# Attention queries loaded without their zeros, and the first weights' clamp on GpSimd

## The chip, the cores and the metric

The kernel runs on one core of a Trainium2 chip. The metric is the device time of one execution in microseconds. The kernel before takes 577.83 us (median of three runs, 577.48 to 578.81).

## The reference

Eight batches go through an attention with a local mask and then through a layer that mixes tokens and channels.

```python
B, H, S, D = 8, 8, 576, 64
scores = q @ k.T / sqrt(D)          # per batch and head
mask: heads 0-3: 0 <= i - j < 32;  heads 4-7: 0 <= i - j < 128 and (i - j) % 4 == 0
attn = softmax(where(mask, scores, -1e9));  o = attn @ v
x = o.transpose(0, 2, 1, 3).reshape(B, S, 512)
theta = x @ w_theta                 # 512 x 512
zr, zi = x * cos(theta), x * sin(theta)
u = x + (w_tok_r @ zr + w_tok_i @ zi)   # over the 576 tokens
out = u + max(u @ w_ch, 0)
```

The mixing weights come as 64-bit numbers and are turned into float32 on the chip.

## The kernel before, in words

**Tiling.** The eight heads of a batch are handled as four pairs. The heads with the dilated mask have their tokens reordered on the host, so that every head sees a window of 32 tokens. A pair's 576 queries are 18 blocks of 32; a block of queries meets the 64 keys of its own block and the one before. One score matmul does a block for both heads of the pair: the keys of the two heads lie on partitions 0 to 63 and 64 to 127, 64 columns of them stream, and the stationary operand is a tile of 128 partitions by 64 columns that holds head 0's 32 queries in its upper left quarter, head 1's in its lower right quarter, and zeros elsewhere. The result has the queries of the two heads on 64 partitions, and even and odd blocks use the two halves of the array's columns. In float32 each matmul becomes two instructions of TensorE, and each of them a weight load (PEld) and a stream (PE), so a pair has 36 of each.

**The zeros.** The host writes the zeros into the array qT (1001 to 1010), and every load of a pair's queries brings them along: 128 partitions by 1152 numbers, 576 KB, of which half are zeros. The queries of batch 0 go into four tiles that are later used for something else (278, 282); those of the other batches into a pool of two buffers (218, 221), 28 loads of them.

**Weights.** `unpack` (311 to 345) makes float32 of a 64-bit weight tile, whose 32-bit halves lie interleaved, so that each operation steps 8 bytes: a clamp of the upper half on VectorE (332), a scaling on ScalarE (334), a shift or scaling of the lower half (337 or 340), and a merge on VectorE (342). `split` (347) then makes a high part on ScalarE and a low part on GpSimd (352). The weights that are unpacked with `early` set are the four tiles of w_theta (st_wth) and the five of the first half of the token weights (st_wtk, g = 0). The second token half and w_ch come later, with `early` false.

**The stages.** Batch 0's attention comes first, then theta (667), the cosines and sines, and the token and channel units (850, 882). From batch 1 on, a batch's token and channel matmuls run beside the next batch's scores (468), probabilities (504 to 510), transposes (525), products with v (617) and theta (685). The low parts `zl` of the rotated tokens (646) are made on GpSimd.

**Order.** The work of batch 0 and the beginning of batch 1 is put in order by a small planner (`Order`, 62 to 125): each step names an engine and a cost in ns, and steps of a lower rank go first. The engines run what it emits in that order, each in its own queue. So a cost or an engine that a step names also moves the steps around it. From batch 1's units on, the order is written out by hand (`phase`, 889) and doesn't depend on costs. All loads and stores are issued by SyncE (SP), one after the other.

Of the kernel before, what the change touches and what calls it, by code (L numbers as in the profile page):

```python
# [8 lines left out]
F32 = mybir.dt.float32  # L9
# [5 lines left out]
ALU = mybir.AluOpType  # L15
PSUM = bass.MemoryType.PSUM

B, H, S, D = 8, 8, 576, 64
DM = H * D
NP = H // 2  # L20
QB = 32
BW = 2 * QB
NJ = S // (2 * QB)
# [35 lines left out]
W_MAX = 2.0 ** 16 * (2.0 - 2.0 ** -3)  # L59


class Order:
# [13 lines left out]
    def pin(self, ins):  # L76
        if self.live:
            self.tc.keep_in_program_order(ins)

    def signal(self, event):  # L80
        self.events[event] = self.now
# [53 lines left out]
def dve2(n):  # L135
    return 67 + 0.52 * n


def act(n):
    return 95 + 0.83 * n  # L140
# [6 lines left out]
def dma(n):  # L147
    return 128 * 4 * n / 360.0
# [3 lines left out]
def build(ctx, tc, qT, kT, vw, wth, wtk, wch, maskb, ident, identb, outT):  # L152
    nc = tc.nc
    cp = ctx.enter_context(tc.tile_pool(name="const", bufs=1))
    ap = ctx.enter_context(tc.tile_pool(name="attn", bufs=2))
# [12 lines left out]
    pin, go, signal = od.pin, od.go, od.signal  # L168

    def pe(ins):  # L170
        tc.keep_in_program_order(ins)
# [17 lines left out]
    def take(tag, bufs, n=None):  # L189
        n = reserve(tag) if n is None else n  # L190
        if od.live:
            if n >= bufs:
                yield None, ("free", tag, n - bufs)
            if n:
                yield None, ("got", tag, n - 1)
            signal(("got", tag, n))
        return n
# [15 lines left out]
    def load_qk(n):  # L213
        if n >= B * NP:
            return
        b, pr = divmod(n, NP)
        r = yield from take("qk", 2)
        q = ap.tile([128, 2 * NJ, 2 * QB], F32, tag="q", name=f"q{b}_{pr}")
        k = ap.tile([128, S + 32], F32, tag="k", name=f"k{b}_{pr}")
        yield "DMA", dma(2 * S)  # L220
        pin(nc.sync.dma_start(q, qT[b, pr]))
        yield "DMA", dma(S + 32)
        pin(nc.sync.dma_start(k, kT[b, pr]))
        qks[b, pr] = (q, k, r)
        signal(("qk", b, pr))

    def load_va(n):
        if n >= B * NP:
            return
        b, pr = divmod(n, NP)  # L230
        r = yield from take("va", 2)
        va = ap.tile([128, VA, 128], F32, tag="va", name=f"va{b}_{pr}")
        yield "DMA", dma(VA * 128)
        pin(nc.sync.dma_start(va, vw[b, pr, :, :VA]))
        vs["a", b, pr] = (va, r)
        signal(("va", b, pr))

    def load_vb(n):
# [12 lines left out]
        vs["b", b, pr] = (vb, r)  # L251
        signal(("vb", b, pr))

    KE = S + 32
    first_k = hp.tile([128, 10 * HS], F32R, tag="wt_b", name="first_k").bitcast(F32)
    first_v = hp.tile([128, 8 * HS], F32R, tag="wt_a", name="first_v").bitcast(F32)
# [13 lines left out]
    def first_loads():  # L270
        yield "DMA", dma(3 * BW + 64)
        pin(nc.sync.dma_start(mskb, maskb.bitcast(BF16)))
        pin(nc.sync.dma_start(idb, identb.bitcast(BF16)))
        for pr in range(NP):
            yield from take(f"xh{pr}", 1, 0)
            yield from take(f"u{pr}", 1, 0)
            pqs.append(hp.tile([128, 2, S], F32R, tag=f"xh{pr}", name=f"P0_{pr}").bitcast(F32)[:, 0])
            q = hp.tile([128, 2, S], F32R, tag=f"u{pr}", name=f"q0_{pr}").bitcast(F32)
            q = q.rearrange("p a b -> p (a b)").rearrange("p (a b) -> p a b", b=2 * QB)
            k = first_k[:, KE * pr:KE * pr + KE]  # L280
            yield "DMA", dma(2 * S)
            pin(nc.sync.dma_start(q, qT[0, pr]))
            yield "DMA", dma(KE)
            pin(nc.sync.dma_start(k, kT[0, pr]))
            qks[0, pr] = (q, k, None)
            if pr == 0:
                yield "DMA", dma(128)
                pin(nc.sync.dma_start(idt, ident))
            signal(("qk", 0, pr))
        for pr in range(NP // 2):  # L290
            v = first_v[:, NJ * 128 * pr:NJ * 128 * pr + NJ * 128].rearrange("p (a b) -> p a b", b=128)
            yield "DMA", dma(NJ * 128)
            pin(nc.sync.dma_start(v, vw[0, pr]))
            for h, t in (("a", v[:, :VA]), ("b", v[:, VA:])):
                vs[h, 0, pr] = (t, None)
                signal(("v" + h, 0, pr))
        for pr in range(NP // 2, NP):
            yield from load_va(pr)
            yield from load_vb(pr)

    def consts():
        yield "DVE", 60
        pin(nc.vector.memset(halfpi, math.pi / 2))
        for n in range(2):
            t = cp.tile([128, NJ, 2, 2 * QB], F32, name=f"pt{n}")
            yield "POOL", 1040
            pin(nc.gpsimd.memset(t, 0.0))
            pts.append(t)
        signal("pts")

    def unpack(src, sz, name, stage, early, n, key):

        tag = None
        if stage is None:
            st = hp.tile([128, 2 * DM], F32R, tag=f"wc{n}", name=f"st_{name}{n}")
        else:
            tag = stage
            yield from take(tag[0], 1, tag[1])
            st = hp.tile([128, 2, S], F32R, tag=tag[0], name=f"st_{name}{n}").rearrange("p a b -> p (a b)")
        raw = st[:, :2 * sz].bitcast(U32)  # L320
        yield "DMA", dma(2 * sz)
        if len(src.shape) == 3:
            pin(nc.sync.dma_start(raw.rearrange("p (c b) -> p c b", c=src.shape[1]), src.bitcast(U32)))
        else:
            pin(nc.sync.dma_start(raw, src.bitcast(U32)))
        signal(("raw", name, n))
        yield None, ("raw", name, n)
        pair = raw.rearrange("p (a b) -> p a b", b=2)
        Ci, Ti = pair[:, :, 1], pair[:, :, 0]
        C, T = Ci.bitcast(F32), Ti.bitcast(F32)  # L330
        yield "DVE", dve2(sz)
        pin(nc.vector.tensor_scalar(C, C, W_MAX, -W_MAX, op0=ALU.min, op1=ALU.max))
        yield "ACT", act(sz)
        pin(nc.scalar.activation(C, C, AF.Prelu, scale=2.0 ** -112, alpha=-2.0 ** 32))
        if early and n % 2 == 0:
            yield "DVE", dve2(sz)
            pin(nc.vector.tensor_scalar(Ti, Ti, 29, None, op0=ALU.logical_shift_right))
        else:
            yield "ACT", act(sz)
            pin(nc.scalar.activation(Ti, Ti, AF.Copy, scale=2.0 ** -29, bias=-0.5))  # L340
        yield "DVE", dve(sz)
        pin(nc.vector.scalar_tensor_tensor(out=Ti, in0=Ci, scalar=3, in1=Ti,
                                           op0=ALU.logical_shift_left, op1=ALU.bitwise_or))
        signal(key)
        return T, tag
# [95 lines left out]
    def scores(b, pr):  # L441
# [3 lines left out]
        if pr >= 1:  # L445
            yield None, ("sc", b, pr - 1)
        q, k, rqk = qks[b, pr]
        if b == 0:
            P, rp = pqs[pr].rearrange("p (a b) -> p a b", b=BW), None
        else:  # L450
            rp = yield from take("P", 2)
            P = sp.tile([128, NJ, BW], F32, tag="P", name=f"P{b}_{pr}")
# [3 lines left out]
        for g0, g1 in ((0, 5), (5, NJ)):  # L456
            ps, rel = yield from bank("s", f"s{b}_{pr}_{g0}")
            ps = ps[:, :(g1 - g0) * BW].rearrange("p (a b) -> p a b", b=BW)
            held[g0] = ps, rel
            masked = on_pe(b, pr)  # L460
            if masked:
                yield "PE", 150
                mask_on_pe(ps, pr, g0, g1)
            yield "PE", 162 * (g1 - g0)
            for n in range(g0, g1):
                for e in range(2):
                    qb = 2 * n + e
                    pe(nc.tensor.matmul(ps[64 * e:64 * e + 64, n - g0], q[:, qb],
                                        k[:, QB * qb:QB * qb + BW], start=not masked, stop=not masked or n == g1 - 1))
            if masked:  # L470
                go(row_max(b, ps, rel, P, mx, g0, g1, ("mask", b, pr, g0)))
            else:
                go(mask_scores(ps, rel, P, mx, pr, g0, g1, ("mask", b, pr, g0)))
# [521 lines left out]
def _arrays(inp):  # L995
    import numpy as np
    q, k, v = inp["q"], inp["k"], inp["v"]
# [5 lines left out]
        return a  # L1003

    q, k, v = perm(q), perm(k), perm(v)
    qT = np.zeros((B, NP, 2, D, 2 * NJ, 2, QB), q.dtype)
    qh = q.reshape(B, NP, 2, 2 * NJ, QB, D).transpose(0, 1, 2, 5, 3, 4)
    for hh in range(2):
        qT[:, :, hh, :, :, hh] = qh[:, :, hh]
    qT = qT.reshape(B, NP, 128, 2 * NJ, 2 * QB)  # L1010
    kT = np.zeros((B, NP, 128, S + 32), k.dtype)
    kT[..., 32:] = k.transpose(0, 1, 3, 2).reshape(B, NP, 128, S)
    vp = np.zeros((B, H, S + 32, D), v.dtype)
# [11 lines left out]
    for n, (j, bound) in enumerate(((1, 0), (0, 0), (2, 144), (4, 288), (6, 432), (7, 432))):  # L1025
        for quad in range(4):
            qb = 2 * j + quad // 2
            p = QB * qb + np.arange(QB)[:, None]
# [30 lines left out]
```

## Time and profile before

The profiled execution took 577.82 us, of which the span of its trace is 576.0 us; the 1.82 us around it is start and end.

| | |
|---|---|
| median of the runs | 577.83 us |
| profiled execution | 577.82 us, span 576.0 us, granted TensorE clock 0.988 |
| TensorE | streams 550.5 us (96%), weight loads 501.6 us (87%) |
| VectorE, ScalarE, GpSimd | 378.0, 345.2, 222.2 us |
| DMA | 81.91 MB in 45586 packets, 142 GB/s over the span |

In the rows of the profile, PE is TensorE's stream and PEld its weight load, which overlap; DVE is VectorE, ACT ScalarE, POOL GpSimd, SPq the issue of a DMA by SyncE. A group's row gives line, engine, operation, output<-inputs, shapes and count, then the busy time in us and the mean of one in ns, then the idle time ahead of it and what ended that. A row of the timeline begins with its start and length in us.

### The profile page before, as it was taken

How to read it: one execution, taken by the hardware profiler on the slowest of the kernel's cores; microseconds unless marked ns; L12 is line 12 of the kernel's file. 1: busy time of each engine (PE TensorE's matmuls, PEld its weight loads, DVE VectorE, ACT ScalarE, POOL GpSimd, SP SyncE). 2: the span in 40 equal slices, each digit the busy share in tenths (PEclk: the TensorE clock that was granted, in tenths of full speed). 3: DMA queues.
4: the chain of work that ended last, by engine and by line, in shares of the span. 5: the costliest groups of instructions: out<-in, count | busy, mean ns of one | idle time of the engine just before them, and what ended most of it. 6: DMA issues, size and time to landing. Idle time of an engine off the chain costs nothing.

```text
span 576.0 us, 13996 instructions
## 1 busy us (share of the span) xinstructions
PE 550.5 (96%) x5464; PEld 501.6 (87%) x5464; DVE 378.0 (66%) x1156; ACT 345.2 (60%) x939; POOL 222.2 (39%) x206
## 2 busy tenths in 40 slices
PE   5997799999999999999999999999999999999997
PEld 4744688879999899988999899988999899989997
DVE  3879798865666668756776768756775767445112
ACT  1498967768555784369555785359556695266110
POOL 2228855525224352226324253226323353325220
PEclk9999699899999999999999999999999999999999
DMA  8991437601747046540746146550747123321002
GB/s 303 400 368 28 165 105 245 216 0 63 231 150 193 32 162 210 169 127 20 268 143 172 64 148 202 181 136 11 252 146 190 69 83 102 77 89 65 18 1 83
DMA packets 45586, 81.91 MB, mean 142 GB/s; under 512 B 3920, under 2 KB 19024, under 8 KB 45520
## 3 DMA queue, kind: packets, MB, share of 16 engines
q1 hardware_dynamic: 45520, 81.02, 43.7%
q8 instruction: 43, 0.70, 0.5%
q14 instruction: 23, 0.19, 0.1%
HBM read 64.49 MB, written 16.52 MB: 141 GB/s over the span
## 4 chain that ended last, share of the span: by engine, by line
DVE 34%; ACT 30%; PE 25%; issue 5%; POOL 2%; DMA 2%; SPq 0%; ACTq 0%; POOLq 0%; DVEq 0%
DVE pt L525 16%; PE y L850 11%; ACT P L504 11%; PE c L882 6%; PE th L685 3%; DVE P L409 3%; ACT K L698 3%; ACT K L787 3%; DVE xh L599 3%; ACT th L796 2%; ACT zh L644 2%; DVE xq L729 2%; DVE K L789 2%; ACT cos L705 2%; ACT x L581 2%
## 5 line engine op out<-in xcount | busy, mean ns | idle before, releaser
L830 POOL TENSOR_TENSOR u<-x,u 128x288 fp32r<-128x288 f32 x64 | 54.7, 858 | 184.6 <-ACT u L828 184.6
L525 DVE STREAM_TRANSPOSE pt<-P 32x288 f32<-32x288 f32 x224 | 105.1, 469 | 12.0 <-POOL P L510 8.9
L882 PE MATMUL c<-u,late_wc 128*128 128x288 f32 x768 | 110.2, 296 | 2.8 <-DVE x L859 2.8
L882 PEld LDWEIGHTS c<-u,late_wc 128*128 128x128 f32 x768 | 106.0, 188 | 6.8 <-DVE x L859 4.0
L850 PE MATMUL y<-wtkh,zh 128*128 128x288 f32 x288 | 90.3, 314 | 1.1 <-ACT zh L644 1.1
L850 PE MATMUL y<-wtkh,zl 128*128 128x288 f32 x288 | 86.2, 299 | 4.0 <-POOL zl L646 4.0
L646 POOL TENSOR_TENSOR zl<-g,zh 128x512 fp32r<-128x512 f32 x40 | 52.3, 1316 | 97.5 <-ACT zh L644 84.5
L504 ACT ACTIVATE P<-P,mx 128x64 f32<-128x64 f32 x216 | 72.0, 335 | 25.8 <-DVE mx L498 25.8
L850 PE MATMUL y<-wtkl,zh 128*128 128x288 f32 x288 | 85.9, 298 | 0.0
L828 ACT CAST u<-x 128x288 fp32r<-128x288 f32 x64 | 26.9, 429 | 86.2 <-DVE x L825 85.5
L685 PE MATMUL th<-wthh,xh 128*128 128x512 f32 x224 | 74.8, 395 | 0.3 <-DVE g L784 0.3
L850 PE MATMUL y<-late_wt_b,zh 128*128 128x288 f32 x320 | 68.1, 297 | 0.0
L825 DVE TENSOR_TENSOR x<-y,x 128x288 f32<-128x288 f32 x64 | 28.1, 448 | 53.6 <-PE y L850 53.5
L850 PEld LDWEIGHTS y<-wtkh,zl 128*128 128x128 f32 x288 | 55.1, 191 | 4.7 <-POOL zl L646 4.7
L850 PEld LDWEIGHTS y<-wtkh,zh 128*128 128x128 f32 x288 | 54.9, 191 | 4.7 <-ACT zh L644 2.3
L850 PE MATMUL y<-late_wt_a,zh 128*128 128x288 f32 x256 | 56.3, 301 | 0.0
L850 PEld LDWEIGHTS y<-wtkl,zh 128*128 128x128 f32 x288 | 55.1, 191 | 0.3 <-issue 0.3
L510 POOL TENSOR_TENSOR P<-P,sm 128x576 f32<-128x576 f32 x32 | 37.5, 1172 | 41.1 <-DVE sm L508 18.1
L850 PEld LDWEIGHTS y<-late_wt_b,zh 128*128 128x128 f32 x320 | 51.4, 189 | 0.3
L685 PEld LDWEIGHTS th<-wthh,xh 128*128 128x128 f32 x224 | 42.0, 188 | 9.2 <-DVE g L784 0.6
L850 PE MATMUL y<-late_wt_b,zl 128*128 128x288 f32 x160 | 47.4, 296 | 0.0
L581 ACT COPY x<-o 128x576 f32<-128x576 f32 x32 | 29.4, 919 | 28.4 <-PE o L617 19.1
(108 smaller groups left out, 1106.3 us busy)
## 6 DMA issues: line engine op xcount, KB each, us to landing
q<-in_qT_dram SPq DMA_DIRECT2D x32, 576.0 KB, 5.2
va<-in_vw_dram SPq DMA_DIRECT2D x30, 320.0 KB, 3.2
k<-in_kT_dram SPq DMA_DIRECT2D x28, 304.0 KB, 5.5
out_dram<-x SPq DMA_DIRECT2D x28, 288.0 KB, 2.4
vb<-in_vw_dram SPq DMA_DIRECT2D x29, 256.0 KB, 3.8
xd<-xq SPq DMA_DIRECT2D x24, 288.0 KB, 5.1
xn<-xd SPq DMA_DIRECT2D x24, 256.0 KB, 3.4
st_wtk<-in_wtk_dram SPq DMA_DIRECT2D x8, 576.0 KB, 8.8
```

Source lines behind the costliest of these rows:

```text
L409: pin(nc.vector.tensor_tensor_reduce(out=P[:, n], in0=ps[:, n - g0], in1=mskb[:, mask_of(pr, n)], op0=ALU.add, op1=ALU.max, scale=1.0, sca ...
L504: table(nc.scalar.activation(P[:, n], P[:, n], AF.Exp, bias=mx[:, n:n + 1], scale=SCALE, accum_out=sm[:, n:n + 1]))
L510: pin(nc.gpsimd.tensor_tensor(P, P, sm.unsqueeze(2).to_broadcast([128, NJ, BW]), op=ALU.mult))
L525: pin(nc.vector.transpose(pmats[b, pr][k0:k0 + QB, :, hh, QB * e:QB * e + QB], P[p0:p0 + QB, :, QB * o:QB * o + QB]))
L581: pin(nc.scalar.copy(dst, src))
L646: pin(nc.gpsimd.tensor_tensor(lo, z, hi.bitcast(F32), op=ALU.subtract))
L685: pe(nc.tensor.matmul(pt, l, r, start=(n == 0), stop=(n == 3 * NC - 1)))
L825: pin(nc.vector.tensor_tensor(x[:, ts], ps, x[:, ts], op=ALU.add))
L828: pin(nc.scalar.copy(uh[b, d][:, ts], x[:, ts]))
L830: pin(nc.gpsimd.tensor_tensor(ul[b, d][:, ts], x[:, ts], uh[b, d][:, ts].bitcast(F32), op=ALU.subtract))
L850: pe(nc.tensor.matmul(ps, l[:, cs], r, start=(n == 0), stop=(n == 3 * NK - 1)))
L882: pe(nc.tensor.matmul(ps, l[:, cs], r[:, ts], start=(n == 0), stop=(n == 3 * NC - 1)))
```

## The change

It has two parts.

**Queries.** The host writes qT without zeros. A head's row holds for each of its 64 dimensions the 576 queries in the order "place in the block, then block". A pair's load is now two DMAs of 64 partitions by 576 numbers, one for each head, and each goes to its own half of a tile of 128 by 2 by 576. The other half of either partition range is set to zero by a memset: for batch 0's four tiles by VectorE just ahead of the loads, for two tiles that are now kept for all other batches by GpSimd, once. The score matmul's stationary operand is column `qb` of every group of 18: 64 columns that lie 72 bytes apart, where they were next to each other before.

**Clamp.** In `unpack`, the clamp of the nine early tiles is done by GpSimd with the planner's cost 1.2 ns an element, and no longer by VectorE.

```diff
 def load_qk(n):
-        q = ap.tile([128, 2 * NJ, 2 * QB], F32, tag="q", name=f"q{b}_{pr}")
+        q = qbufs[r % 2]
         k = ap.tile([128, S + 32], F32, tag="k", name=f"k{b}_{pr}")
-        yield "DMA", dma(2 * S)
-        pin(nc.sync.dma_start(q, qT[b, pr]))
+        yield "DMA", dma(S)
+        for hh in range(2):
+            rs = slice(64 * hh, 64 * hh + 64)
+            pin(nc.sync.dma_start(q[rs, hh], qT[b, pr, rs]))
...
+    qbufs = [cp.tile([128, 2, S], F32, name=f"q{n}") for n in range(2)]
...
 def first_loads():
-            q = q.rearrange("p a b -> p (a b)").rearrange("p (a b) -> p a b", b=2 * QB)
+            for hh in range(2):
+                pin(nc.vector.memset(q[64 * hh:64 * hh + 64, 1 - hh], 0.0))
-            yield "DMA", dma(2 * S)
-            pin(nc.sync.dma_start(q, qT[0, pr]))
+            yield "DMA", dma(S)
+            for hh in range(2):
+                rs = slice(64 * hh, 64 * hh + 64)
+                pin(nc.sync.dma_start(q[rs, hh], qT[0, pr, rs]))
...
 def consts():
         signal("pts")
+        for q in qbufs:
+            for hh in range(2):
+                yield "POOL", 580
+                pin(nc.gpsimd.memset(q[64 * hh:64 * hh + 64, 1 - hh], 0.0))
...
 def unpack(src, sz, name, stage, early, n, key):
-        yield "DVE", dve2(sz)
-        pin(nc.vector.tensor_scalar(C, C, W_MAX, -W_MAX, op0=ALU.min, op1=ALU.max))
+        if early:
+            yield "POOL", 1.2 * sz
+            pin(nc.gpsimd.tensor_scalar(C, C, W_MAX, -W_MAX, op0=ALU.min, op1=ALU.max))
+        else:
+            yield "DVE", dve2(sz)
+            pin(nc.vector.tensor_scalar(C, C, W_MAX, -W_MAX, op0=ALU.min, op1=ALU.max))
...
 def scores(b, pr):
         q, k, rqk = qks[b, pr]
+        q = q.rearrange("p h (r n) -> p (h r) n", n=2 * NJ)
...
-                    pe(nc.tensor.matmul(ps[64 * e:64 * e + 64, n - g0], q[:, qb],
+                    pe(nc.tensor.matmul(ps[64 * e:64 * e + 64, n - g0], q[:, :, qb],
...
 def _arrays(inp):
+    qT = q.reshape(B, H, 2 * NJ, QB, D).transpose(0, 1, 4, 3, 2).reshape(B, NP, 128, S)
```

How the rows move is seen at three places. The first is GpSimd's queue from its first multiplications of probabilities on (P; the number after the name is the pair, the last one only a serial number). Before:

```order
L307 MEMSET pt_109 128x1152
L510 ISA
L510 TENSOR_TENSOR P_0_104<-P_0_104,sm_0_117 128x576
L510 TENSOR_TENSOR P_1_114<-P_1_114,sm_1_148 128x576
L510 TENSOR_TENSOR P_2_121<-P_2_121,sm_2_183 128x576
L510 TENSOR_TENSOR P_3_154<-P_3_154,sm_3_227 128x576
L352 TENSOR_TENSOR wtkl_516<-st_wtk_0_149,wtkh_515 128x576
```

Now, with the change's own line numbers (323 is the memset of the kept query tiles, 347 the clamp, 529 the multiplication, 370 the low part):

```order
L317 MEMSET pt_112 128x1152
L323 MEMSET q_90 64x576 x2
L323 MEMSET q_91 64x576 x2
L529 TENSOR_TENSOR P_1_118<-P_1_118,sm_1_167 128x576
L347 TENSOR_SCALAR st_wth_98<-st_wth_98 128x512
L529 TENSOR_TENSOR P_2_129<-P_2_129,sm_2_202 128x576
L347 TENSOR_SCALAR st_wth_99<-st_wth_99 128x512
L529 TENSOR_TENSOR P_3_152<-P_3_152,sm_3_246 128x576
L347 TENSOR_SCALAR st_wth_100<-st_wth_100 128x512
L347 TENSOR_SCALAR st_wth_101<-st_wth_101 128x512
L347 TENSOR_SCALAR st_wtk_0_168<-st_wtk_0_168 128x576
```

Clamps now stand between the multiplications of the pairs, and each waits in this queue for its tile's DMA.

The second place is VectorE's queue behind the last pair's scores of batch 0, before:

```order
L332 TENSOR_SCALAR st_wth_96<-st_wth_96 128x512
L495 TENSOR_REDUCE sm_3_227<-P_3_154 128x9
L536 COPY pt_107<-pT_2_0_355 64x10x32
L536 COPY pt_107<-pT_2_5_389 64x8x32
L337 TENSOR_SCALAR st_wth_96<-st_wth_96 128x512
L507 TENSOR_SCALAR sm_3_227<-sm_3_227 128x9
L508 RECIPROCAL sm_3_227<-sm_3_227 128x9
L342 SCALAR_TENSOR_TENSOR st_wth_96<-st_wth_96 128x512
L332 TENSOR_SCALAR st_wth_97<-st_wth_97 128x512
L332 TENSOR_SCALAR st_wth_98<-st_wth_98 128x512
```

And now (355 is the shift, 360 the merge, 514 the sum of a row):

```order
L355 TENSOR_SCALAR st_wth_98<-st_wth_98 128x512
L360 SCALAR_TENSOR_TENSOR st_wth_98<-st_wth_98 128x512
L514 TENSOR_REDUCE sm_3_246<-P_3_152 128x9
L555 COPY pt_110<-pT_2_0_375 64x10x32
L526 TENSOR_SCALAR sm_3_246<-sm_3_246 128x9
L527 RECIPROCAL sm_3_246<-sm_3_246 128x9
L555 COPY pt_110<-pT_2_5_413 64x8x32
L360 SCALAR_TENSOR_TENSOR st_wth_99<-st_wth_99 128x512
```

The clamps are gone, and the first weight tile's merge stands ahead of the last pair's sum.

The third place is the head of SyncE's queue. Before:

```order
L282 DMA q_0_105<-in_qT_dram 128x1152
L284 DMA first_k<-in_kT_dram 128x608
L288 DMA idt<-in_ident_dram 128x128
L282 DMA q_1_115<-in_qT_dram 128x1152
L284 DMA first_k<-in_kT_dram 128x608
```

Now:

```order
L292 DMA q_0_106<-in_qT_dram 64x576 x2
L294 DMA first_k<-in_kT_dram 128x608
L298 DMA idt<-in_ident_dram 128x128
L292 DMA q_1_119<-in_qT_dram 64x576 x2
L294 DMA first_k<-in_kT_dram 128x608
```

The order of the tiles stays, and two smaller DMAs stand for each load of queries.

More of the change, by code (lines that the diff above doesn't have):

```diff
@@ L1005, in _arrays @@
     q, k, v = perm(q), perm(k), perm(v)
[L1006 to L1010, printed above, removed]
+    qT = q.reshape(B, H, 2 * NJ, QB, D).transpose(0, 1, 4, 3, 2).reshape(B, NP, 128, S)
     kT = np.zeros((B, NP, 128, S + 32), k.dtype)
```

## The prediction

> **What bounds the kernel now.** The page's first part and its row of DMA come first, then the busy time by stretches (length, then PE, PEld, DVE, ACT, POOL, with the granted clock, the share of DMA and GB/s at the end).
>
> ```profile
> PE 550.5 (96%) x5464; PEld 501.6 (87%) x5464; DVE 378.0 (66%) x1156; ACT 345.2 (60%) x939; POOL 222.2 (39%) x206
> DMA  8991437601747046540746146550747123321002
> ```
>
> ```profile
> 0.00:20.00 20.00, 12.88 (x220) 10.58 (x220) 8.40 (x23) 3.52 (x6) 4.38 (x8) 1.00 0.89 330
> 20.00:40.00 20.00, 18.14 (x259) 10.71 (x260) 16.04 (x34) 15.29 (x26) 4.72 (x5) 1.00 1.04 398
> 40.00:60.00 20.00, 16.09 (x86) 8.62 (x84) 18.83 (x43) 17.83 (x32) 14.79 (x11) 0.94 0.29 96
> ...
> 62.00:143.00 81.00, 74.44 (x694) 66.73 (x692) 63.44 (x145) 61.49 (x183) 44.22 (x38) 0.94 0.36 121
> 143.00:508.40 365.40, 362.62 (x3729) 341.07 (x3729) 248.23 (x868) 223.06 (x655) 134.11 (x129) 1.00 0.47 142
> ```
>
> Two kernels lie behind one average. From 143 us on TensorE is busy 362.6 of 365.4 us, and the others have a third free: only what TensorE itself does counts there. Before that it waits. DMA is full for 40 us, VectorE is busy 18.83 of 20 us from 40 to 60, ScalarE 17.83. The chain that ended last, in its first part, names the steps.
>
> ```profile
> 3.53 6.60 DMA first_k<-in_kT_dram
> ...
> 23.41 0.82 DVE st_wth L332
> ...
> 26.94 1.30 DVE st_wth L332
> ...
> 32.59 0.41 DVE st_wth L332
> ```
>
> A load of keys holds the start up to 10.13 us, and three pieces of the clamp (line 332) lie on the chain, 0.82 + 1.30 + 0.41 = 2.53 us. So the change touches both regimes: loads and clamps in the start, and the stationary operand of the scores where TensorE is the bound. The sums are made against the profiled execution, 577.82 us (span 576.0, 1.82 around it); the median of the runs, 577.83, is the same.
>
> **Term 1, the first loads.** The DMA view (KB each, then us to landing) and the timeline:
>
> ```profile
> q<-in_qT_dram SPq DMA_DIRECT2D x32, 576.0 KB, 5.2
> first_k<-in_kT_dram SPq DMA_DIRECT2D x4, 304.0 KB, 7.3
> idt<-in_ident_dram SPq DMA_DIRECT2D x1, 64.0 KB, 4.5
> ```
>
> ```profile
> 7.03 1.34 PE L468 MATMUL s<-first_k,q 128*64 128x64 f32 x20 [3.62 <-DMA first_k<-in_kT_dram]
> 8.62 1.12 PE L468 MATMUL s<-first_k,q 128*64 128x64 f32 x16
> 10.27 1.34 PE L468 MATMUL s<-first_k,q 128*64 128x64 f32 x20
> ```
>
> From the first pair's keys (scores start at 7.03) to the second's (landed at 10.13) came idt, q and k, 64 + 576 + 304 = 944 KB in 3.1 us, 305 KB a us. Half of a q is 288 KB, 0.94 us. The first scores gain at most that, the second pair's keys twice that, 1.9 us; but TensorE is at the first pair until 9.74, so a second 0.94 can't all be used. Nothing shown moves 64 partitions of q, so the lower end is 0. I take 0.9, the first pair's share, with 0 and 1.9 as ends. SyncE issues one more DMA a pair, some 0.4 us each in the start, beside transfers that are longer.
>
> **Term 2, the clamps.** VectorE loses nine operations:
>
> ```profile
> L332 DVE TENSOR_SCALAR st_wth<-st_wth 128x512 f32<-128x512 f32 x4 | 3.1, 793 | 0.0
> L332 DVE TENSOR_SCALAR st_wtk<-st_wtk 128x576 f32<-128x576 f32 x8 | 5.2, 654 | 0.0
> L332 DVE TENSOR_SCALAR st_wtk<-st_wtk 128x288 f32<-128x288 f32 x2 | 2.9, 1456 | 0.0
> ```
>
> Four of 793 ns, four of 654 and one of at most 1456 are 7.2 us, the upper end of the gain. On the chain they were 2.53 us. What is late next is ScalarE, which follows the clamp with line 334 and has only 20 - 17.83 = 2.17 us free from 40 to 60. So I take 2.0; the lower end is 0, if ScalarE's other work simply fills the place. I assume that what is gained by 60 us is carried to 143 us, since the steps between are the same and hang on one another, and from there to the end, since TensorE then only starts its full stretch earlier.
>
> **What hides at no cost.** The memsets have no row of their own size, so these bound them:
>
> ```profile
> 8.40 0.49 DVE L430 TENSOR_REDUCE mx<-s 128x5 f32<-128x320 f32 x1 [7.54 <-PE s L468]
> 13.67 1.15 POOL L510 TENSOR_TENSOR P<-P,sm 128x576 f32<-128x576 f32 x1 [10.89 <-DVE sm L508]
> L307 POOL MEMSET pt<- 128x1152 f32 x2 | 2.1, 1058 | 0.3 <-POOLq L1045 0.3
> L495 DVE TENSOR_REDUCE sm<-P 128x9 f32<-128x576 f32 x4 | 3.0, 748 | 0.4 <-ACT P L493 0.4
> ```
>
> GpSimd writes zeros at 1058 / 1152 = 0.92 ns a column, 0.53 us for 576. VectorE's eight take 4.2 us by that and 6.0 us at the 748 ns of a whole reduction; VectorE is idle from 0.86 to 8.40, and the first scores need only the first two. GpSimd's four (2.1 us) lie in 10.89 us of idle time. Both cost 0; without that cover, 4 us and 2 us.
>
> GpSimd's nine clamps lie between a memset's rate, 0.47 us for 512, and a two-input operation of the same size:
>
> ```profile
> L646 POOL TENSOR_TENSOR zl<-g,zh 128x512 fp32r<-128x512 f32 x40 | 52.3, 1316 | 97.5 <-ACT zh L644 84.5 <-issue 7.4 <-DVE zh L641 5.6
> L352 POOL TENSOR_TENSOR wtkl<-st_wtk,wtkh 128x576 fp32r<-128x576 f32 x4 | 6.0, 1512 | 10.1 <-ACT wtkh L350 10.1
> ```
>
> They are 4 to 12 us in all. I take 0.7 us each, 6.3 us, nearer the memset, as one operand is read. They come while GpSimd waits, 10.1 us in one piece ahead of line 352, so they cost nothing while the data are there in time; the case where they aren't is a rival.
>
> **Term 3, the stationary operand.** Each of the 28 pairs of batches 1 to 7 has 36 loads, whose columns will lie 72 bytes apart.
>
> ```profile
> L882 PEld LDWEIGHTS c<-u,late_wc 128*128 128x128 f32 x768 | 106.0, 188 | 6.8 <-DVE x L859 4.0
> L617 PEld LDWEIGHTS o<-pt,va 128*64 128x64 f32 x600 | 20.2, 137 | 5.8 <-issue 5.1 <-ACT pt L539 0.8
> L882 PE MATMUL c<-u,late_wc 128*128 128x288 f32 x768 | 110.2, 296 | 2.8 <-DVE x L859 2.8
> L685 PE MATMUL th<-wthh,xh 128*128 128x512 f32 x224 | 74.8, 395 | 0.3 <-DVE g L784 0.3
> ```
>
> ```profile
> 469.01 1.13 PEld L468 LDWEIGHTS s<-k,q 128*64 128x64 f32 x36 [0.16 <-ACT cos L705]
> 155.33 0.64 ACT L581 COPY x<-o 128x576 f32<-128x576 f32 x1 [4.68 <-PE o L617]
> 173.56 1.19 ACT L581 COPY x<-o 128x576 f32<-128x576 f32 x1
> ```
>
> A load of 64 columns less is 188 - 137 = 51 ns shorter, 0.80 ns a column. A stream takes (395 - 296) / (512 - 288) = 0.44 ns a column. The 36 loads start within 1.13 - 0.14 = 0.99 us, every 28.4 ns (the last one's 0.14 taken off), so about two of 51 ns run at a time, and the streams set the pace. No row has columns apart in a stationary operand. TensorE is seen to fetch a number of 4 bytes in 0.44 ns, and a load asks for one in 0.80: a fetch at half the rate would still keep up. On ScalarE the same 576 numbers take 0.64 us when written side by side (pairs 0 and 1) and 1.19 us when written 16 bytes apart (pairs 2 and 3), so something in the memory does cost 1.9 times. The ends are thus 0 and a doubled load; I take 0, since TensorE's own rows are nearer than another engine's write, and keep the other end as the first rival.
>
> The sum: 577.82 - 0.9 - 2.0 + 0 = **574.9 us**. Its own range, with half of term 2's upper end, is 571 to 577.
>
> **Rivals.**
>
> 1. **The loads of apart columns are slower** (ends slower). At 1.9 to 2 times, a load goes from 51 to 102 ns; two at a time give one every 51 ns where 28.4 are needed. That is 22.6 ns x 36 x 28 = 22.8 us, and with terms 1 and 2 the time is 597.7 us. At 1.5 times it is one every 38.2 ns, 9.9 us, and 584.8. The point from which it decides is a load of over 2 x 28.4 = 57 ns, 12% more than now. For it: ScalarE's row, and that TensorE has no slack after 143 us. Against it: the stream's 0.44 ns. The page "SBUF — State Buffer" of the Trainium skill, section "Door 1: The DMA port swizzle", says that memory lines are 16 bytes, that two hits on a line are needed for the full rate, and that each access to a new line pays. By that rule the loads pay here and this rival's time holds; ScalarE's 1.19 against 0.64 us agrees with it for writes, and no run shows yet a load of weights.
>
> 2. **The start doesn't move** (about as before, 577.8). Two halves of 64 partitions could take as long as the whole did, term 1 is 0, and ScalarE fills what the clamps leave. For it: ScalarE's 17.83 of 20. Against it: DMA moves half the bytes, and the clamps lay on the chain. The same page, section "Can I just issue two DMAs to hit both halves?", says that two DMAs on the two halves of the partitions go one after the other at half the ports, which gives term 1 as 0 and 575.8 us.
>
> 3. **GpSimd's queue runs late.** The first two clamps now stand ahead of the multiplications of pairs 2 and 3.
>
> ```profile
> 11.62 0.33 SPq L325 DMA_DIRECT2D st_wth<-in_wth_dram  x1
> 22.80 1.15 POOL L510 TENSOR_TENSOR P<-P,sm 128x576 f32<-128x576 f32 x1 [2.62 <-ACT pt L539]
> st_wth<-in_wth_dram SPq DMA_DIRECT2D x4, 512.0 KB, 9.8
> ```
>
> The first weight tile is issued at 11.62 and lands 9.8 us later, at 21.4; its clamp ends at 22.1 by my price and 22.7 by the upper one, against 22.80 for the multiplication. With a landing 2 us later the chain of pairs 2 and 3 is 2 us late twice and the gain is lost: 577.82 - 2.9 + 4 = 578.9 at most.
>
> **How the numbers follow.** The forecast 0.52; the slower loads 0.33; no movement 0.10; the late queue 0.05. I predict 574.9. About 0.2% (1.2 us) is what a measurement of this kernel can tell from no change. Faster is the forecast, 0.52; same is rival 2, 0.10; slower is rivals 1 and 3, 0.38. Cases of both signs hold most of the chance, so the range must reach over both: 571 (term 1 whole, term 2 at 5) to 598 (doubled loads). Outside are loads that no longer overlap (102 - 28.4 ns x 36 x 28 = 74 us more) and a start that gains 7 us or more, together some 0.1.
>
> **What would show it.** Right: the weight loads of the scores still near 138 ns and 36 of them within 1.13 us; the full stretch of TensorE from before 141 us; the first scores at 6.1 us; no clamp of st_wth on VectorE, ScalarE's line 334 earlier. Wrong: 36 loads of scores that need 1.4 to 2 us and some 0.8 us more of TensorE a pair; first scores at 7.0 as before; a multiplication of P that waits for a DMA behind a clamp; VectorE's or ScalarE's idle time from 20 to 60 us grown by what was taken out.

## The result, and the profile after

The changed kernel takes 603.06 us (median of four runs, 602.84 to 603.35), the kernel before 577.65 (four runs, 576.67 to 578.81). The ratio is 1.0433 with a 95% interval from 1.0409 to 1.0457. The profiled execution took 603.09 us, its span is 601.1 at a granted clock of 0.985, where the kernel before had 0.988, so the clock isn't the cause. The prediction was 574.9, and its range ended at 598.

First come the busy time, the row of DMA and the engines of the chain that ended last, from the page of the changed kernel.

```profile
PE 578.4 (96%) x5464; PEld 530.5 (88%) x5464; DVE 379.8 (63%) x1155; ACT 348.2 (58%) x939; POOL 230.5 (38%) x219
DMA  8993136501537135451547134560546222241102
PE 81%; DVE 8%; DMA 5%; ACT 3%; issue 1%; SPq 1%; POOL 1%; DVEq 0%; POOLq 0%
```

The chain of the kernel before was shared by three engines:

```profile
DVE 34%; ACT 30%; PE 25%; issue 5%; POOL 2%; DMA 2%; SPq 0%; ACTq 0%; POOLq 0%; DVEq 0%
```

TensorE has 27.9 us more to do (578.4 for 550.5, with the same 5464 instructions), and the chain now runs through it for 81% of the span. By stretches, in the columns of the prediction:

```profile
0.00:20.00 20.00, 13.55 (x220) 11.54 (x220) 12.75 (x31) 3.47 (x6) 6.79 (x12) 0.91 0.86 273
20.00:40.00 20.00, 19.27 (x267) 11.52 (x264) 13.63 (x26) 15.80 (x26) 10.92 (x12) 1.00 1.04 346
62.00:143.00 81.00, 73.96 (x686) 66.91 (x686) 57.90 (x142) 57.21 (x175) 40.73 (x36) 0.92 0.31 98
145.50:530.00 384.50, 384.50 (x3738) 364.45 (x3737) 251.92 (x870) 227.72 (x659) 135.96 (x130) 1.00 0.41 118
```

In the full stretch TensorE no longer has any idle time; before, it had 2.8 us (365.40 less 362.62). Which instructions grew is told by the groups of the scores: stream and weight load of before, then of the changed kernel (busy us and mean ns behind the bar).

```profile
L468 PE MATMUL s<-k,q 128*64 128x64 f32 x1008 | 37.5, 229 | 0.0
L468 PEld LDWEIGHTS s<-k,q 128*64 128x64 f32 x1008 | 33.7, 143 | 3.7 <-issue 2.0 <-ACT cos L705 0.8 <-DVE g L750 0.8
```

```profile
L487 PE MATMUL s<-k,q 128*64 128x64 f32 x1008 | 65.0, 284 | 0.0
L487 PEld LDWEIGHTS s<-k,q 128*64 128x64 f32 x1008 | 61.2, 210 | 4.2 <-issue 2.4 <-DVE K L808 0.8 <-PE th L686 0.8
```

The 1008 loads of 28 pairs went from 143 to 210 ns, and the streams that wait for them from 37.5 to 65.0 us: 27.5 of the 27.9 us are here. The 144 streams of batch 0 (first_k), whose columns are apart too, went from 8.9 to 10.3 us. One pair in the timeline of the changed kernel:

```profile
293.51 2.16 PEld L487 LDWEIGHTS s<-k,q 128*64 128x64 f32 x36
305.51 2.18 PEld L487 LDWEIGHTS s<-k,q 128*64 128x64 f32 x36
```

With the last one's 0.21 taken off, a load starts every (2.17 - 0.21) / 35 = 56 ns, where the prediction had read 28.4 ns from the row of before.

The end of batch 1's last theta matmuls is a mark in both traces that splits the span:

```profile
137.86 0.39 PE L685 MATMUL th<-wthh,xh 128*128 128x512 f32 x1
```

```profile
145.47 0.39 PE L704 MATMUL th<-wthh,xh 128*128 128x512 f32 x1
```

The start is 7.6 us longer, and the rest (576.0 - 137.86 = 438.1; 601.1 - 145.47 = 455.6) 17.5. So there is a loss in either part. The experiments separate the causes. They also show how the mark moves in single executions; a microsecond or two of it can be chance, since the kernel before alone ran between 575.55 and 580.35 us in the batches of runs below.

### The profile page after: what moved, and what is told of

Its sections match the earlier page's. It is cut to its first block, busy times and chain, and to the rows that moved or that the text cites. A ratio compares the mean times of both kernels' runs of the same rounds, so it can differ in the third digit from the quotient of the medians.

```text
span 601.1 us, 14039 instructions
## 1 busy us (share of the span) xinstructions
PE 578.4 (96%) x5464; PEld 530.5 (88%) x5464; DVE 379.8 (63%) x1155; ACT 348.2 (58%) x939; POOL 230.5 (38%) x219
## 2 busy tenths in 40 slices
DMA packets 46098, 72.48 MB, mean 121 GB/s; under 512 B 4432, under 2 KB 19536, under 8 KB 46032
## 4 chain that ended last, share of the span: by engine, by line
PE 81%; DVE 8%; DMA 5%; ACT 3%; issue 1%; SPq 1%; POOL 1%; DVEq 0%; POOLq 0%
PE y L869 35%; PE c L901 16%; PE th L704 12%; PE s L487 9%; PE o L636 5%; DVE pt L544 3%; DMA st_wtk<-in_wtk_dram 2%; DMA q<-in_qT_dram 1%; DVE st_wtk L360 1%; DMA st_wch<-in_wch_dram 1%; PE th L709 1%; ACT P L523 1%; DMA first_k<-in_kT_dram 1%; PE th L708 1%; DVE st_wch L360 1%
## 5 line engine op out<-in xcount | busy, mean ns | idle before, releaser
L487 PE MATMUL s<-k,q 128*64 128x64 f32 x1008 | 65.0, 284 | 0.0
L487 PEld LDWEIGHTS s<-k,q 128*64 128x64 f32 x1008 | 61.2, 210 | 4.2 <-issue 2.4
## 6 DMA issues: line engine op xcount, KB each, us to landing
st_wtk<-in_wtk_dram SPq DMA_DIRECT2D x8, 576.0 KB, 8.0
```

What stands on the lines that cost most here:

```text
L487: pe(nc.tensor.matmul(ps[64 * e:64 * e + 64, n - g0], q[:, :, qb], k[:, QB * qb:QB * qb + BW], start=not masked, stop=not masked or n == g ...
```

## The experiments

Each kernel was timed beside the kernel before on the same chip; the ratio is to that one, with its 95% interval. The mark is the one above, from one execution.

| kernel | us (runs) | ratio | mark, rest |
|---|---|---|---|
| e1_side_by_side | 582.34 (4) | 1.0090 [1.0061, 1.0119] | 141.8, 437.0 |
| e2_apart_in_before | 598.61 (4) | 1.0367 [1.0342, 1.0393] | 140.0, 456.8 |
| e3_clamp_only | 582.71 (4) | 1.0091 [1.0067, 1.0115] | 142.2, 438.6 |
| e4_queries_only | 601.03 (4) | 1.0410 [1.0383, 1.0436] | 142.4, 457.8 |
| e5_clamp_pool_old_plan | 578.11 (10) | 1.0014 [0.9995, 1.0032] | 137.7, 438.5 |
| e6_clamp_dve_new_plan | 583.12 (4) | 1.0105 [1.0074, 1.0135] | 141.6, 438.6 |
| e7_step2 | 580.41 (9) | 1.0042 [1.0019, 1.0065] | 138.3, 439.2 |
| e8_step3 | 588.37 (1) | | 139.6, 447.0 |
| e9_step2_old_plan | 581.40 (6) | 1.0051 [1.0036, 1.0065] | 142.7, 438.0 |
| e10_step2_clamp_pool | 581.41 (6) | 1.0054 [1.0037, 1.0070] | 140.7, 438.3 |
| e11_step6 | 598.86 (1) | | 140.2, 456.9 |
| e12_loads_old_plan | 579.08 (11) | 1.0019 [1.0004, 1.0034] | 139.6, 437.9 |

### The distance between the columns

e1 takes the distance out of the changed kernel, e2 puts it alone into the kernel before.

```diff
 e1, in scores of the changed kernel
-        q = q.rearrange("p h (r n) -> p (h r) n", n=2 * NJ)
+        q = q.rearrange("p h s -> p (h s)").rearrange("p (n c) -> p c n", c=2 * QB)
 e2, in scores of the kernel before
+        q = q.rearrange("p a b -> p (a b)").rearrange("p (c n) -> p c n", n=2 * NJ)
...
-                    pe(nc.tensor.matmul(ps[64 * e:64 * e + 64, n - g0], q[:, qb],
+                    pe(nc.tensor.matmul(ps[64 * e:64 * e + 64, n - g0], q[:, :, qb],
```

> The changed kernel with one thing altered: the score matmul's stationary operand is 64 neighbouring columns of the same query tile (64 qb to 64 qb + 63) and no longer 64 columns that lie 72 bytes apart. The scores are then those of mixed-up queries; loads, memsets, clamps and every instruction's size stay. Theory A (the apart columns slow the weight loads): 36 loads of a pair start within about 1.0 us again, a load lasts 138 ns in the median and not 211, and the time is 574 to 578 us. Theory B (the time comes from the start: halves of 64 partitions, the fuller GpSimd queue, a new order by the planner): still 595 us or more.

> The kernel before with one thing altered: the stationary operand is taken as every 18th column of its query tile, so the scores are those of mixed-up queries; zeros, loads and clamps are as before. Theory A: loads of 211 ns, 36 of them in 2.18 us, and 600 to 606 us. Theory B: 577 to 579 us.

The weight loads of the 28 pairs, e1 and then e2:

```profile
L487 PEld LDWEIGHTS s<-k,q 128*64 128x64 f32 x1008 | 32.6, 139 | 4.2 <-issue 1.8 <-ACT cos L724 0.8 <-PE th L686 0.8
```

```profile
L469 PEld LDWEIGHTS s<-k,q 128*64 128x64 f32 x1008 | 61.0, 210 | 3.6 <-issue 2.8 <-DVE g L751 0.8
```

Without the distance 603.06 becomes 582.34, 20.7 us less; with the distance alone 577.18 (the kernel before in that batch) becomes 598.61, 21.4 more. The two agree, so the distance costs 21 us by itself, whatever loads and clamps do. Both kernels differ from their partner in the address of the stationary operand alone. The loads are as theory A had them, the times are not: e1 stays above its 574 to 578 us, since 5 us of the loss are something else, and e2 comes out below its 600 to 606.

e7, e8 and e11 vary the distance; e8 and e11 were run once each. The queries of a pair are laid out in groups of two, three or six blocks, so that the 64 columns of a block lie 8, 12 or 24 bytes apart; all three compute the reference's scores. Planner and clamps are those of e4.

```diff
+QS = 2          # e8: 3, e11: 6
...
-            pin(nc.sync.dma_start(q[rs, hh], qT[b, pr, rs]))
+            qv = q.rearrange("p h s -> p (h s)").rearrange("p (g h x) -> p g h x", h=2, x=QB * QS)
+            pin(nc.sync.dma_start(qv[rs, :, hh], qT[b, pr, rs].rearrange("p (g x) -> p g x", x=QB * QS)))
...
-        q = q.rearrange("p h (r n) -> p (h r) n", n=2 * NJ)
+        q = q.rearrange("p h s -> p (h s)").rearrange("p (g c i) -> p g c i", c=2 * QB, i=QS)
...
-                    pe(nc.tensor.matmul(ps[64 * e:64 * e + 64, n - g0], q[:, :, qb],
+                    pe(nc.tensor.matmul(ps[64 * e:64 * e + 64, n - g0], q[:, qb // QS, :, qb % QS],
```

> Queries without zeros, correct result, clamps on VectorE; a query tile holds its blocks in twos, so that the columns of a stationary operand lie 8 bytes apart (runs of 256 bytes in the loads' destination). Theory L (a line of 16 bytes with two hits is free): loads of 138 ns, 36 in 1.13 us, 576 to 579 us. Theory P (any step over 4 bytes pays): loads near 211 ns, about 600 us. Short runs in the loads could add a few us in the first 40 us under either.

> The same with blocks in threes, columns 12 bytes apart: 64 columns lie on 48 lines, 1.33 to a line. Theory L: between, some 165 to 190 ns a load, 585 to 592 us. Theory P: as 72 bytes, about 600 us.

> As e7_step2, with blocks in groups of six, so that the columns of a stationary operand lie 24 bytes apart (planner as in e4_queries_only, clamps on VectorE). Theory (what counts is whether two neighbouring columns share 16 bytes; beyond that the distance doesn't matter): 36 loads in 2.1 to 2.2 us, a load near 210 ns, 599 to 602 us as e4_queries_only. Rival (the price grows with the distance, 1.17 us at 8 bytes, 1.68 at 12, 2.17 at 72): 36 loads in 1.75 to 2.0 us and 590 to 597 us.

The groups of the weight loads at 8, 12 and 24 bytes:

```profile
L488 PEld LDWEIGHTS s<-k,q 128*64 128x64 f32 x1008 | 34.2, 142 | 4.1 <-issue 1.9 <-DVE K L809 1.1 <-ACT cos L725 0.8
```

```profile
L488 PEld LDWEIGHTS s<-k,q 128*64 128x64 f32 x1008 | 48.0, 177 | 4.2 <-issue 3.1 <-DVE K L809 1.1
```

```profile
L488 PEld LDWEIGHTS s<-k,q 128*64 128x64 f32 x1008 | 60.2, 207 | 4.2 <-issue 3.1 <-DVE K L809 1.1
```

And one pair of each in the timeline:

```profile
476.44 1.17 PEld L488 LDWEIGHTS s<-k,q 128*64 128x64 f32 x36
```

```profile
484.99 1.68 PEld L488 LDWEIGHTS s<-k,q 128*64 128x64 f32 x36
```

```profile
488.01 2.14 PEld L488 LDWEIGHTS s<-k,q 128*64 128x64 f32 x36 [0.16 <-issue]
```

From one load's start to the next these are (1.17 - 0.14) / 35 = 29 ns, (1.68 - 0.18) / 35 = 43 ns and (2.14 - 0.21) / 35 = 55 ns; at 4 bytes it was 28.4 and at 72 it is 56. From 24 to 72 bytes hardly more is lost, so e11's rival, a price that grows with the distance, falls. The 598.86 us of e11 are just below the 599 to 602 that the theory gave, in one run. e8 is where theory L had it; e7's loads are too, but its 580.41 us lie 1.4 above the theory's range, which is taken up under the loads of queries. The steps fit a count of pieces of 16 bytes that the 64 columns touch: 16 pieces at 4 bytes, 32 at 8, 48 at 12 and 64 at 24 or 72. 43 / 48 is 0.90 ns and 55 / 64 is 0.86 ns a piece; 32 pieces would by that be some 28 ns, as much as the streams take anyway, and so 8 bytes are nearly free. Pieces of 8 bytes would number 64 at 8, 12 and 24 bytes alike, and pieces of 32 bytes 24 at 12, 48 at 24 and 64 at 72; neither goes with 29, 43, 55 and 56 ns. The count is a fit to five distances and not seen in the trace itself. This is the rule that the prediction drew from the Trainium skill, "SBUF — State Buffer", section "Door 1: The DMA port swizzle": two hits on a 16-byte line give the full rate, and less pays. The trace agrees on weight loads: two columns to a line cost 142 ns a load, one column 207 to 210.

Time follows the loads less than in full. From e7 to e8 the group grows by 13.8 us and the time by 8.0; from e8 to e11 by 12.2 and 10.5. The difference goes in part into waits that TensorE had anyway: behind the mark its idle time is 5.6 us in e7 and 3.4 in e8.

### The clamps and the planner

e3 is the clamp part of the change alone. e5 has the clamps on GpSimd with the planner told VectorE's old cost; e6 has them on VectorE with the planner told GpSimd's.

```diff
 e3, in unpack of the kernel before
-        yield "DVE", dve2(sz)
-        pin(nc.vector.tensor_scalar(C, C, W_MAX, -W_MAX, op0=ALU.min, op1=ALU.max))
+        if early:
+            yield "POOL", 1.2 * sz
+            pin(nc.gpsimd.tensor_scalar(C, C, W_MAX, -W_MAX, op0=ALU.min, op1=ALU.max))
...
 e5: the old yield, and the new engine
         yield "DVE", dve2(sz)
+        eng = nc.gpsimd if early else nc.vector
+        pin(eng.tensor_scalar(C, C, W_MAX, -W_MAX, op0=ALU.min, op1=ALU.max))
 e6: the new yield, and the old engine
+            yield "POOL", 1.2 * sz
+            pin(nc.vector.tensor_scalar(C, C, W_MAX, -W_MAX, op0=ALU.min, op1=ALU.max))
```

> The kernel before with the early weights' clamp on GpSimd, queries as before. If the clamps were on the path that sets the end, as the prediction took it, about 2 us faster: 575 to 576.5 us. If ScalarE or the loads fill the place, 577 to 578.5 us. If GpSimd's queue holds up the multiplications, 578.5 to 580 us.

> The kernel before; the early clamps run on GpSimd, but the planner is still told VectorE and VectorE's cost, so every other engine keeps its order of before. Theory C (GpSimd's own work costs the 5.5 us of the clamp alone: it takes long, and its port holds up VectorE's merges): 581 to 584 us. Theory D (the new order that the planner makes of it costs them): 575 to 578 us.

> The mirror of it: the early clamps stay on VectorE, but the planner is told GpSimd and 1.2 ns an element. Theory C: 577 to 579 us. Theory D: 581 to 585 us, the more so as VectorE still has the work.

e3 loses 5.5 us (582.71 against 577.18), more than any of the three cases had it. e5, with the same operation on the same engine, is within its interval of no change; e6, which leaves the operation where it was, loses 5.1 (583.12 against 577.97). So the clamp's engine is worth nothing that these runs can tell, and the number that the planner is told costs 5 us, by the order that follows from it. The 5 us that were left in e1 are of this size. They are no fixed price: beside the queries' part the clamps with their order cost 2.0 us by the medians (601.03 in e4, 603.06 in the changed kernel) and 1.3 by the ratios, where they cost 5.5 alone.

Why the engine is worth nothing is seen from 20 to 60 us, before and then e5:

```profile
20.00:60.00 40.00, 34.23 (x344) 19.33 (x344) 34.87 (x76) 33.12 (x57) 19.51 (x15) 0.97 0.67 247
```

```profile
20.00:60.00 40.00, 34.23 (x344) 19.45 (x344) 29.52 (x67) 32.80 (x57) 25.23 (x24) 0.97 0.67 247
```

VectorE does 5.4 us less, and TensorE's 34.23 us don't change. The chain of e5, at the place where before's had its clamps:

```profile
26.48 1.40 POOL P L511
27.88 0.63 POOL st_wth L333
...
33.83 7.24 DMA st_wtk<-in_wtk_dram
```

The second clamp starts at 27.9 behind a multiplication of probabilities on GpSimd, where before's began at 26.9 on VectorE, and the load of the token weights was issued at 33.8 in both traces (33.86 before) and holds the chain to 41.1. By these rows the clamps lay on one of several chains of nearly the same length.

What the new order does shows at TensorE's longest wait after the start. In order: before, e5, e3, e6.

```profile
101.51 0.30 PE L424 MATMUL s<-mskb,idb 128*128 128x64 bf16 x2 [1.95 <-ACT P L485]
```

```profile
101.63 0.30 PE L425 MATMUL s<-mskb,idb 128*128 128x64 bf16 x2 [1.96 <-ACT P L486]
```

```profile
105.08 0.43 PE L428 MATMUL s<-mskb,idb 128*128 128x64 bf16 x2 [4.02 <-ACT P L489]
```

```profile
105.26 0.43 PE L428 MATMUL s<-mskb,idb 128*128 128x64 bf16 x2 [3.32 <-ACT P L489]
```

The same scores start 3.6 to 3.8 us later with the new order, 1.4 to 2.1 us of it in this wait. Which of the moved steps is the cause wasn't tried.

### The loads of queries

e4 is the changed kernel with all clamps on VectorE. e9 and e10 are e7's layout with before's costs told to the planner, so that all engines' order is that of before; e10 has the early clamps on GpSimd besides. e12 has the change's own loads and memsets, in rows of 2304 bytes, with before's costs and order, clamps on VectorE and no distance.

```diff
 e9, against e7; e12 likewise, with e1's line in scores
-        yield "DMA", dma(S)
+        yield "DMA", dma(2 * S)
...
-                yield "POOL", 580
 e10, against e9
+        eng = nc.gpsimd if early else nc.vector
-        pin(nc.vector.tensor_scalar(C, C, W_MAX, -W_MAX, op0=ALU.min, op1=ALU.max))
+        pin(eng.tensor_scalar(C, C, W_MAX, -W_MAX, op0=ALU.min, op1=ALU.max))
```

> The changed kernel with all clamps on VectorE again: the queries' part alone. Theory A with a start that gains nothing by the clamp: 603 us as the whole change; with a clamp worth 2 us: 605 us. Theory B with the fault in GpSimd's clamps: 578 us or less.

> Queries without zeros, a block pair's columns 8 bytes apart (as in e7_step2), clamps on VectorE, and the planner is told the costs of before, so that every engine's order is that of before. Theory (what e7 lost, 2.4 us, is the planner's order; the loads themselves give nothing): 576.5 to 579.0 us, ratio 0.998 to 1.002, TensorE's full stretch from 135 to 136 us. Rival a (the loads or the two issues a pair cost it): 580 us or more again, 1.003 to 1.006. Rival b (term 1 of the prediction, hidden in e7 by the new order): 575 to 576.9 us, ratio 0.9985 or less, full stretch from before 134.8 us.

> e9_step2_old_plan with the early clamps on GpSimd, order of before on all other engines: both parts of the change without the 72-byte step and without the new order. Theory (neither part binds): as e9 within 0.2%, 576.5 to 579.0 us. Rival (terms 1 and 2 are there, but each hides the other): 574 to 576 us, ratio 0.997 or less.

> The change's own loads of queries (two DMAs of 64 partitions, rows of 2304 bytes) and memsets, alone: clamps on VectorE, the planner told the costs of before, so that every engine's order is that of before; the stationary operand is 64 neighbouring columns, which are mixed-up queries. Theory (e9's loss is that of its loads in rows of 256 bytes, with 78866 packets for 45586, and of memsets behind the first reduction): 577 to 579.5 us, ratio 0.998 to 1.002, TensorE's full stretch from within 1 us of that of before. Rival a (two DMAs a pair on SyncE's queue and the memsets cost the start it all, whatever their rows): 580 us or more, ratio 1.004 or more, and the full stretch 2 us or more later. Rival b (term 1 of the prediction): 576.9 us or less against 578, ratio 0.998 or less, full stretch 0.7 us or more earlier.

e12 is 1.1 us slower by its ratio (0.2 to 2.0): the theory's range, and no gain from the loads. Its mark is 1.7 us later, between the theory and rival a. e4 against e2 (+2.4 us) and e1 against e3 (-0.4) lie on both sides of it; in these two pairs the order differs as well. e4 itself took 601.03 us, where 603 or 605 were expected. e9 and e10 are as rival a of e9 had it: some 3 us slower by their ratios, and so what e7 lost wasn't the planner's order, against the theory. Their rows of 256 bytes make 78866 packets for 46098 in e12, and on ScalarE the same steps come 1.4 us later than before from 33 us on in e9, 0.2 in e12; that it is the length of the rows wasn't tried apart. e10 shows again that the clamps' engine is worth nothing. None of the kernels beats the kernel before; e5 is the nearest.

The first microseconds show what the loads do: SyncE's issues and the first scores of two pairs, in the changed kernel.

```profile
1.65 1.19 SPq L292 DMA_DIRECT2D q<-in_qT_dram  x2
2.88 0.59 SPq L294 DMA_DIRECT2D first_k<-in_kT_dram  x1
...
8.69 0.58 SPq L294 DMA_DIRECT2D first_k<-in_kT_dram  x1
...
12.16 0.33 SPq L339 DMA_DIRECT2D st_wth<-in_wth_dram  x1
```

```profile
6.29 1.42 PE L487 MATMUL s<-first_k,q 128*64 128x64 f32 x20 [2.83 <-DMA first_k<-in_kT_dram]
9.79 1.38 PE L487 MATMUL s<-first_k,q 128*64 128x64 f32 x20 [0.26 <-DMA first_k<-in_kT_dram]
```

In the kernel before SyncE took 0.42 for a load of queries and sent the last pair's keys off at 6.13:

```profile
1.64 0.42 SPq L282 DMA_DIRECT2D q<-in_qT_dram  x1
...
6.13 0.47 SPq L284 DMA_DIRECT2D first_k<-in_kT_dram  x1
```

The first scores gain 0.74 us and the second pair 0.48. Then the last pair's keys are issued 2.6 us later than before (8.69, 6.13) and the first weight tile 0.5 us later (12.16; the prediction shows 11.62). Fewer bytes also came at a lower rate: 273 for 330 GB/s in the first 20 us, 346 for 398 in the next, while the transfers' share of the time stayed (0.86 for 0.89, then 1.04 in both).

In the order of before, in e9 and e12, VectorE writes the last zeros after its first reductions. In e9:

```profile
9.40 0.43 DVE L448 TENSOR_REDUCE mx<-s 128x4 f32<-128x256 f32 x1 [0.37 <-PE s L487]
9.88 0.54 DVE L290 MEMSET q<- 64x576 f32 x1
10.58 0.54 DVE L290 MEMSET q<- 64x576 f32 x1 [0.16 <-issue]
11.15 0.42 DVE L451 TENSOR_TENSOR P<-s,mx 128x256 f32<-128x256 f32 x1
```

The subtraction of line 451 starts at 11.15; line 433 of the kernel before does it at 10.26, and e12 at 10.78. In the changed kernel the last memset ends at 6.4, and this isn't there.

In e12 none of this lasts: from 40 to 90 us ScalarE's steps come 0.2 us later than in the kernel before. Then one step makes it 1.5 us, the first clamp of w_ch (st_wch), whose load stands behind a load of queries in SyncE's queue. Before, and then e12:

```profile
85.84 0.33 SPq L221 DMA_DIRECT2D q<-in_qT_dram  x1
86.22 2.69 SPq L325 DMA_DIRECT2D st_wch<-in_wch_dram  x2
...
91.07 0.43 DVE L332 TENSOR_SCALAR st_wch<-st_wch 128x512 f32<-128x512 f32 x1
```

```profile
84.20 2.30 SPq L223 DMA_DIRECT2D q<-in_qT_dram  x2
86.61 2.52 SPq L338 DMA_DIRECT2D st_wch<-in_wch_dram  x2
...
92.61 0.43 DVE L345 TENSOR_SCALAR st_wch<-st_wch 128x512 f32<-128x512 f32 x1 [1.38 <-DMA st_wch<-in_wch_dram]
```

The two halves hold the queue for 2.30 us, where the whole took 0.33; the tile is sent off 0.4 us later and the clamp waits 1.38 us for it. This is most of the mark's 1.7 us, read from one execution of each kernel and not tried by itself.

## Why the prediction was wrong, step by step

**Term 3, the stationary operand: the step that failed.** "I take 0, since TensorE's own rows are nearer than another engine's write." It measured 21 us. The 0.44 ns a number came from streams of neighbouring numbers, which say nothing of numbers that lie apart; the only rows with a distance in them were ScalarE's 0.64 and 1.19 us. They have the factor 1.86, and the loads' pace turned out 56 / 28.4 = 1.97 times slower. That the two are so close is in part luck, as 28.4 ns is the streams' pace and not the loads' own; a load itself went from 143 to 210 ns. The nearest row is the one with the same kind of access, not the one of the same engine. The term should have been rival 1's, which had the mechanism and the point from which it decides.

**Rival 1's size.** It gave a load every 51 ns and 22.8 us; the pace is 56 ns, and (56 - 28.4) ns x 36 x 28 = 27.8 us, as the group's row shows (27.5). The time grew by 21, since the waits that TensorE had took some up. Behind the mark lie 22 of the 28 pairs (792 of the 1008 streams). There the streams grew from 27.1 to 50.0 us, 22.9 more, and the stretch by 17.5: TensorE's idle time in it fell from 6.1 to 3.4 us, and nine matmuls of w_ch (line 882), 2.5 us, had moved ahead of the mark. The prediction counted these 28 pairs alone and left out the four of batch 0, which took 1.4 us more. "TensorE has no slack after 143 us" was thus nearly right, and the chain of before (34% VectorE, 30% ScalarE, 25% TensorE) would have said that it wasn't the only bound. The rival's 597.7 also took off the 2.9 us of terms 1 and 2.

**Term 2, the clamps: -2.0 taken, none of it there.** The end at 0 was right. That an operation lies on the one chain that ended last doesn't make its time a gain, when chains of the same length run beside it. What was not priced is the order: the text before the prediction shows steps that change places because a cost changed, and the prediction counted these at nothing. They cost 5.1 us (e6) by themselves, more than the 2.9 of terms 1 and 2. Rival 3 looked for such a loss in GpSimd's queue, and it isn't there:

```profile
21.29 0.65 POOL L347 TENSOR_SCALAR st_wth<-st_wth 128x512 f32<-128x512 f32 x1 [1.43 <-DMA st_wth<-in_wth_dram]
22.64 1.15 POOL L529 TENSOR_TENSOR P<-P,sm 128x576 f32<-128x576 f32 x1 [0.70 <-ACT pt L558]
```

The clamp waits 1.43 us for its tile, as the rival had it, and still the multiplication behind it starts at 22.64, for 22.80 before, since it was waiting for ScalarE until then.

**Term 1, the first loads: -0.9 taken, -0.4 (e1 against e3) and +1.1 (e12) measured.** The first scores come at 6.29, near the forecast's 6.1, but the gain isn't carried on. The step that failed is "SyncE issues one more DMA a pair, some 0.4 us each in the start, beside transfers that are longer": a half takes 0.55 to 0.6 us, and the keys' issue went from 0.47 to 0.58. In e12 the second pair's keys are issued at 5.14, for 3.53 before, and landed 5.00 us later, at 10.14, for 10.13: the transfer gained 1.6 us and the queue lost as much. The rest of e12's loss lies at 90 us, in the same queue. That SyncE's queue is what took the gain back is read from these rows and was not tried by itself. Rival 2 cited the Trainium skill, "SBUF — State Buffer", section "Can I just issue two DMAs to hit both halves?", by which two halves go one after the other. The 273 and 346 GB/s at nearly the share of before agree with it, but no run sets two halves against one whole alone.

**What hides at no cost: right.** The memsets took 0.54 us on VectorE and 572 ns on GpSimd, in idle time; GpSimd's clamps of 512 columns took 646 ns for the 0.7 us assumed.

The sum, in the order of the kernels run, by their medians: 577.65 before; the planner's order with the clamps +5.1 (582.71, e3); the loads -0.4 (582.34, e1); the distance +20.7 (603.06). In another order the parts are of other sizes: the queries' part first is +23.4 (601.03, e4), and the clamps with their order then +2.0.

## What to carry to other kernels

Before the elements of a stationary operand are put apart to save bytes, count how many lie within 16 bytes: two or more kept the loads' pace here, four on three pieces made the time from load to load 1.5 times as long, one twice as long. Take a price from the row with the same access pattern, even if another engine made it. And where a planner's costs set the order, run the new order with the old operation by itself: the number may cost more than the operation, and not the same beside another change.

## What was not expected of the hardware

A weight load of 64 columns in float32 took 143 ns at 4 bytes apart, 142 at 8, 177 at 12, 207 at 24 and 210 at 72. SyncE took 0.55 to 0.6 us to issue a load for 64 partitions by 576 numbers, more than the 0.42 for 128 by 1152, so two halves cost 1.1 to 1.2 us of its queue.
